# Issue order at the start of a fused RWKV-7 and gated-cosine kernel: loads, first chunks and one chunk's segments

## The chip, the core and the metric

The kernel runs on one core of one Trainium2 chip. Its metric is the device time of one execution, in microseconds (us). A core has TensorE for matrix products and transposes (PE in the profile, PEld for its weight loads), VectorE (DVE), ScalarE (ACT), GpSimd (POOL) and SyncE (SP, which here only issues DMA transfers). Each engine works through its own instruction list in program order, and engines wait for each other by semaphores.

## What is computed

A linear-attention recurrence over 768 tokens, and behind it a feed-forward layer with the activation h cos(h):

```python
batch, n_heads, seq, head_dim = (4, 8, 768, 40)
for t in range(S):
    y[:, :, t] = einsum('bhd,bhde->bhe', rt, state)
    Sa = einsum('bhde,bhe->bhd', state, at)
    state_decay = state * wt[:, :, None, :] - einsum('bhd,bhe->bhde', Sa, bt)
    state = state_decay + einsum('bhd,bhe->bhde', vt, kt)
# y, as 3072 tokens of 320 numbers, is x
h = x @ w_in            # 320 x 2048
g = h * cos(h)
out = g @ w_out         # 2048 x 320
```

All inputs r, k, v, w, a, b are float32; the two weight matrices arrive as 64-bit numbers.

## The kernel before

The sequence is cut into 24 chunks of 32 tokens; a chunk of all four batches fills 128 partitions. Inside a chunk the recurrence is solved in closed form, from chunk to chunk a state `qz` is carried.

For a chunk c there are these pieces of work, each a function whose instructions are spread over the engines:

- `p1_w`, `p1_a`, `p1_b`, `p1_n` take chunks two at a time. They transpose w, a and b on TensorE (tiles wT, aps, bT), take running products of w (for the first four chunks by a scan on VectorE, later from a scan over four chunks, `ws_scan`, that goes through DRAM as `wd`), divide b by w (`over_w`: a reciprocal on VectorE, a product into `bn` on GpSimd) and form the products of a and b (nps, evacuated to `nt`).
- Every four chunks a triangular inverse is taken from `nt` on VectorE in many short steps (tiles `inv`, `inv_tmp`, `u`). `inv` is first filled on GpSimd with zeros and a diagonal of -1. For chunks 0 to 7 it is inverted as two diagonal blocks, and `pair_first`, `pair_second` add the off-diagonal block with TensorE (tile below).
- `p2_in` and `p2_kn` copy v, r and k of a chunk into padded tiles on GpSimd (vp, rp, kn, vvm); `p2_v`, `p2_k`, `p2_g` transpose them on TensorE (vT, kT) and form the gram products (gram).
- `ch_t`, `ch_q`, `ch_x`, `ch_s`, `ch_z` (t, q, x, s, z below) carry the state through the chunk: transposes of it (sT), products (qps, x0ps, sps, dps) and in z its update and the output yt. `tokens` stores yt to DRAM (xd) and fetches it back transposed (xT) for the feed-forward layer.
- The feed-forward layer runs over pairs of chunks and quarters of the 2048 columns: `first_a`, `first_b` (tile ph), then the cosine (turns, gT), and `second` (tile po). These pieces are put between the others wherever a segment list has M.

The weights are first turned from 64-bit to 32-bit numbers in 20 blocks of 128 x 512 (`rounded`): a fetch of 512 KB (words), `taken` (L243, L244 on VectorE, L247, L249 on ScalarE), `mantissa` (L253 on VectorE, L256 on ScalarE) and `product` (L259 on VectorE, a sign product L262 on GpSimd). These are queued as `w_steps`, four for each block.

The order of everything is written out by hand. `step(work, of_inv, of_w)` runs a segment, then what `later(n, ...)` had set to follow n steps on (mostly loads), then so many inverse steps and weight steps. `busy(n)` and `kept_busy(n)` issue products of zeros on TensorE that nobody reads. The last part of the kernel is one loop over chunks with a list `segs` for each; before it stands the start, chunks 0 to 3, as straight code.

All loads in question go out on SyncE's queue. A load of one input of one chunk is four DMAs of 40 KB in rows of 160 bytes. k, v and r have one tile each, so the loads of chunk c + 1 wait for the copies of chunk c on GpSimd (`landed`); w, a and b alternate between two tiles from chunk 4 on. A DMA on this queue also waits for the one that used the same of eight semaphores before it.

The lines that matter for the change and the prediction, in the start:

Of the kernel before, what the change touches and what calls it, by code (L numbers as in the profile page):

```python
# [9 lines left out]
F32 = mybir.dt.float32  # L10
# [10 lines left out]
def kernel(  # L21
# [43 lines left out]
    nc = tc.nc  # L65
# [269 lines left out]
    G = {"rest": []}  # L335
# [98 lines left out]
    def p1_n(c):  # L434
        ps = at("nps")
        for i in range(2):
            for j in range(4):
                for bb in range(B):
                    for e in range(2):
                        mm(  # L440
                            ps[blk[bb ^ e], e, (4 * i + j) * C : (4 * i + j + 1) * C],
                            G["bT", c + i][half[e], j, blk[bb]], G["aT", c + i][half[e], j, blk[bb]],
                            i == 0 and j == 0,
                        )

        if c % 4 == 0:
            G["nt"] = sb1.tile([P, C, 4, 2, HH], F32, tag="nt", name="nt")
            if c < 8:
                G["noff"] = sb2.tile([P, 4, 2, HH, C], F32, tag="rt", name="noff")
        for e in range(2):  # L450
            nc.scalar.copy(
                G["nt"][:, :, c % 4 : c % 4 + 2, e, :].rearrange("p t c j -> p c j t"),
                ps[:, e, : 2 * HH * C].rearrange("p (c j t) -> p c j t", c=2, j=HH),
            )
        if c < 8:
            for e in range(2):
                nc.scalar.copy(
                    G["noff"][:, c % 4 : c % 4 + 2, e, :, :].rearrange("p c j t -> p c (j t)"),
                    ps[:, e, : 2 * HH * C].rearrange("p (c n) -> p c n", c=2),
                )  # L460
        if c % 4 == 2:
            G["inv"] = sb1.tile([P, C * C], F32, tag="inv", name="inv")
            nc.gpsimd.memset(G["inv"], 0.0)
            nc.gpsimd.memset(G["inv"][:, :: C + 1], -1.0)


    def inv_start():

# [397 lines left out]
    def p1(c):  # L866


        def first_w():
            p1_w(c)  # L870
            if c == 4:
                later(1, lambda: load(6, "w"))

        def both_a():
            p1_a(c)
            if c == 4:
                later(1, lambda: load(7, "w"))
                for i in range(2):
                    later(1, lambda i=i: load(6 + i, "ab"))
            elif c > 4 and c + 3 < NCH:  # L880
                for m in range(6):
                    later((9 if c == 6 else 2) + m, lambda m=m: load(c + 2 + m % 2, "wab"[m // 2]))

        return [first_w, both_a, lambda: p1_b(c), lambda: p1_n(c)]
# [8 lines left out]
    def p2(c):  # L893
        def last():
            p2_g(c)
            if c + 1 < NCH:
                later(1, lambda: p2_in(c + 1))

        return [lambda: p2_v(c), lambda: p2_k(c), last]

# [8 lines left out]
    with tc.manual_schedule():  # L909
# [56 lines left out]
        first, other = p1(0), p1(2)  # L966
        for seg in first[:2]:
            step(seg)
        load(4, "ab")
        load(5, "a")  # L970
        for seg in (*other[:2], *first[2:], *other[2:]):
            step(seg)
        for m in range(2):
            w_work[m][0]()
        scanned(1)
        p2_in(0)
        p2_kn(0)
        inv_steps.extend(by_blocks(0))
        v, k, g = p2(0)
        v1, k1, g1 = p2(1)  # L980
        x0, s0, z0 = main(0)[2:]
        for n, seg, idle_n in ((6, v, 0), (0, k, 0), (0, g, 4), (4, x0, 6), (2, v1, 5)):
            for _ in range(n):
                inv_steps.pop(0)()
            step(seg)
            if seg is x0:
                w_work[2][0]()
                p2_kn(1)
            busy(idle_n)
# [5 lines left out]
        step(g1)  # L995
        busy(3)
        N_PAD = {0: 0, 19: 75}
        step(lambda: pair_first(0, 0, False))
        for m in range(3, 5):
            w_work[m][0]()  # L1000
        step(lambda: pair_second(0, 0, False), 0, 1)
        step(s0, 0, 3)
        busy(6)
        step(z0, 0, 4)
        busy(4)
        for n, c, name in ((3, 4, "w"), (5, 5, "w"), (7, 5, "b")):
            later(n, lambda c=c, name=name: load(c, name))
# [19 lines left out]
        for c in range(NCH):  # L1027
            t, q, x, s, z = main(c)
            v, k, g = p2(c + 1) if c + 1 < NCH else [lambda: None] * 3
            q0 = c - c % 4 + 4  # L1030
            fill, pn, pn4 = (1, 4), None, None
            if c == 0:
                segs = []
            elif c == 1:
                segs, fill = [t, F1, v, q, k, S1, x, g, s, z], (1, 4)
            elif c == 2:
                segs, fill = [t, F2, v, q, S2, k, M, x, M, F3, g, M, s, S3, M, z, M, M], (0, 2)
            elif c == 3:
                pw4, pa4, pb4, pn4 = p1(4)
                pw, pa, pb, pn = p1(6)  # L1040
                segs = [
                    t, pw4, M, q, pa4, M, x, lambda: scanned(2), M, s, pw, M, pb4, pa, M, pn4, M, z, M,
                    pb, v, pn, k, M, g,
                ]
                fill = (2, 3)
            elif c == 4:
                pw, pa, *p8 = p1(8)
                firsts = [lambda n=n: pair_first(4, n) for n in range(4)]
                seconds = [lambda n=n: pair_second(4, n) for n in range(4)]
                F4, F5, F6, F7 = firsts  # L1050
                S4, S5, S6, S7 = seconds
                segs = [
                    t, v, M, q, M, k, x, M, F4, M, S4, F5, M, s, F6, M, pw, F7, M, z, M, g, M, pa, S5, lambda: scanned(3),
                ]
                fill = (2, 0)
            elif c == 5:
                pw, pa = p1(10)[:2]
                pb, pn = p8
                segs = [t, M, pb, q, M, pn, k, M, x, M, s, S6, M, pw, v, M, z, S7, M, g, M, pa, M]
            elif c % 4 == 0 and q0 < NCH:  # L1060
                pb, pn = p1(q0)[2:]
                segs = [t, v, M, q, M, k, x, M, g, M, s, pb, M, z, M, pn, M, M]
                if q0 + 4 < NCH:
                    segs.insert(-1, lambda: scanned(c // 4 + 2))
            elif c % 4 == 1 and q0 < NCH:
                pw, pa = p1(q0 + 2)[:2]
                segs = [t, M, pw, q, M, x, k, M, s, v, M, z, M, pa, M, g, M, M]
            elif c % 4 == 2 and q0 < NCH:
                pb, pn = p1(q0 + 2)[2:]
                segs = [t, M, pb, q, M, pn, v, M, x, M, s, k, M, g, M, z, M, M]  # L1070
            elif c % 4 == 3 and q0 + 4 < NCH:
                pw, pa = p1(q0 + 4)[:2]
                segs = [t, M, pw, q, M, x, k, M, s, v, M, z, M, pa, M, g, M, M]
            else:
                segs = [t, v, M, q, M, x, k, M, g, M, s, M, M, z, M, M]
            n = len(segs)

            goal = 8 * (c + 1) - (18 if c < 19 else 20)
            empty, places = 0, segs.count(M)
            if c > 3:  # L1080
                empty = max(0, min(places - (goal - done), 2 if c < 8 else places))
                goal = max(goal, done + places - empty)
            place = 0
            if c == 19:
                shifted(N_PAD[c])
            for i, seg in enumerate(segs):
                kept_busy(FILL.get((c, i), 0))
                while seg is s and ("rt", c) not in G:
                    if allowed(c):
                        piece(4, 0)  # L1090
                    else:
                        inv_steps.pop(0)()
                while seg is pn4 and w_steps:
                    w_steps.pop(0)()
                if seg is not M:
                    step(seg, *((0, 0) if c < 3 and seg in (*firsts, *seconds) else fill), small=seg in (q, x, g, s, z, pn, pn4, *firsts, *seconds))
                    if seg not in (*firsts, *seconds) and (c < 2 or c == 2 and not done):
                        busy({s: 6, q: 5, v: 4, k: 4, z: 4}.get(seg, 3))
                else:
                    place += 1  # L1100
                    if place * empty // places > (place - 1) * empty // places:
                        continue
                    if allowed(c) and (c != 4 or done < 23):
                        piece(*fill)
                while i == n - 1 and c > 3 and done < goal and c != 4 and allowed(c):
                    piece(*fill)
                if seg is pn and (c == 3 or c > 4 and c % 4 == 2):
                    inv_steps.extend(by_blocks(q0) if c == 3 else inverse(q0))
# [36 lines left out]
```

## Time and profile before

| | us |
|---|---|
| median of three runs | 814.49 |
| lowest and highest | 811.71, 815.9 |
| the profiled execution | 814.53 |
| its span in the trace | 812.8 |
| TensorE busy in the span | 758.7 (93%) |
| VectorE, ScalarE, GpSimd busy | 485.8, 387.1, 199.4 |
| granted TensorE clock, mean | 0.975 |

The span is what the trace covers; the execution is 1.7 us longer. Times in the profile are from the span's start. The page's row of DMA queues:

```profile
q1 hardware_dynamic: 180560, 51.95, 29.5%
q8 instruction: 140, 2.29, 1.2%
```

Columns: packets, megabytes, share of the time of 16 DMA engines. A row of a timeline gives start, length, engine, line, operation, tile written and tiles read, shape and count; in brackets stands how long the engine had been idle before, and who released it. A row of a table of stretches gives the stretch, its length, busy time and number of instructions of each engine, then the granted TensorE clock, the DMA share and GB/s.

### The profile page before, as it was taken

Reading aid. Unit: us, or ns where it says so; the run is one execution under the profiler, and the core shown is the slowest. Engines: PE = TensorE matmul, PEld = TensorE weight load, DVE = VectorE, ACT = ScalarE, POOL = GpSimd, SP = SyncE. Lnnn points to the kernel's source line nnn. Section 1 sums busy time; section 2 is a strip of 40 time slices with the busy share of each in tenths; the row PEclk is TensorE's granted clock in tenths of the full one; section 3 lists DMA queues with packets and bytes.
Section 4 is the critical chain, followed back from the end, with each engine's and each line's share of the span. In section 5 each row is a group of like instructions: output and inputs, shape, how many; then the busy total and the mean of one; then the engine's idle time right before and its main releaser. Section 6 shows DMA issues by size and latency. Waiting matters only on the chain.

```text
span 812.8 us, 39682 instructions
## 1 busy us (share of the span) xinstructions
PE 758.7 (93%) x17859; PEld 582.0 (72%) x17859; DVE 485.8 (60%) x1025; ACT 387.1 (48%) x723; POOL 199.4 (25%) x354
## 2 busy tenths in 40 slices
PE   3678799799999999999999999999999999999997
PEld 2545477677777777777777777777777777777775
DVE  6948858855743797553895554994346873332231
ACT  1326577454454346446436535534635445363352
POOL 5215634330404230230330330331130222201000
PEclk9878699999999999999999999999999999999999
DMA  8656553344244324324214314223220212101000
GB/s 123 120 142 170 158 141 99 54 114 67 51 94 92 67 42 72 69 89 70 59 36 74 78 47 71 55 45 68 45 45 21 45 37 57 23 14 36 19 17 16
DMA packets 183304, 55.79 MB, mean 69 GB/s; under 512 B 157152, under 2 KB 178656, under 8 KB 183136
## 3 DMA queue, kind: packets, MB, share of 16 engines
q1 hardware_dynamic: 180560, 51.95, 29.5%
q8 instruction: 140, 2.29, 1.2%
q10 hardware_dynamic: 2320, 0.98, 0.6%
q0 software_dynamic: 256, 0.33, 0.2%
q14 instruction: 28, 0.23, 0.1%
HBM read 42.07 MB, written 11.14 MB: 65 GB/s over the span
## 4 chain that ended last, share of the span: by engine, by line
PE 68%; DVE 15%; DMA 4%; issue 4%; ACT 4%; SPq 3%; POOL 1%; DVEq 0%; ACTq 0%; POOLq 0%
PE ph L101 23%; PE po L101 19%; PE x0ps L101 4%; PE dps L101 3%; DVE inv_tmp L478 3%; SPq L152 3%; PE gram L101 3%; DVE inv L482 3%; PE vT L328 2%; DVE rw L393 2%; PE sps L101 2%; PE busy L101 2%; PE nps L101 2%; PE qps L101 2%; PE sT L638 1%
## 5 line engine op out<-in xcount | busy, mean ns | idle before, releaser
L101 PE MATMUL po<-w_out_sb,gT 128*128 128x320 f32 x768 | 223.3, 439 | 0.0
L101 PE MATMUL ph<-xT,w_in_sb 128*128 128x256 f32 x768 | 186.7, 388 | 1.5 <-DMA xT<-xd 1.5
L101 PEld LDWEIGHTS po<-w_out_sb,gT 128*128 128x128 f32 x768 | 140.2, 190 | 54.2 <-issue 1.7
L101 PEld LDWEIGHTS ph<-xT,w_in_sb 128*128 128x128 f32 x768 | 140.5, 191 | 30.0 <-issue 10.6
L810 ACT ACTIVATE turns<-ph,rnd 128x512 f32<-128x512 f32 x96 | 64.1, 686 | 151.7 <-PE ph L101 151.3
L812 DVE SCALAR_TENSOR_TENSOR turns<-turns,ph 128x512 f32<-128x512 f32 x96 | 64.0, 684 | 116.0 <-ACT turns L810 115.8
L820 DVE TENSOR_TENSOR gT<-ph,turns 128x512 f32<-128x512 f32 x96 | 65.8, 686 | 37.8 <-ACT turns L817 37.8
L737 POOL TENSOR_TENSOR qz<-qz,wc 128x160 f32<-128x160 f32 x92 | 42.0, 475 | 158.5 <-DVE qz L736 157.9
L817 ACT ACTIVATE turns<-turns,half_pi 128x512 f32<-128x512 f32 x96 | 69.3, 722 | 3.1
L816 ACT ACTIVATE turns<-turns 128x512 f32<-128x512 f32 x96 | 60.1, 627 | 19.1 <-DVE turns L812 19.1
L101 PE MATMUL ph<-xT,w_in_tail 64*128 64x256 f32 x384 | 54.7, 402 | 0.0
L482 DVE TENSOR_TENSOR inv<-inv,inv_tmp 128x31 f32<-128x31 f32 (+15 forms) x124 | 51.2, 413 | 4.3
L570 POOL COPY vp<-nat_v 128x320 f32<-128x320 f32 x24 | 11.7, 489 | 164.4 <-DMA nat_v<-in_v_dram 121.1
L478 DVE TENSOR_TENSOR inv_tmp<-u,inv 128x31 f32<-128x31 f32 (+15 forms) x124 | 48.5, 391 | 2.3
L736 DVE TENSOR_TENSOR qz<-dps,qz 128x160 f32<-128x160 f32 x92 | 29.1, 316 | 33.3 <-PE dps L101 33.2
L393 DVE RECIPROCAL rw<-nat_w 128x320 f32<-128x320 f32 x20 | 42.8, 2142 | 0.0
L642 ACT COPY s<-sT 128x512 f32<-128x512 f32 x46 | 24.5, 585 | 37.8 <-PE sT L638 37.8
L101 PEld LDWEIGHTS ph<-xT,w_in_tail 64*128 64x128 f32 x384 | 33.3, 186 | 9.3 <-issue 5.6
L101 PEld LDWEIGHTS <-idle 32*64 32x64 bf16 (+2 forms) x443 | 21.5, 101 | 24.3 <-issue 19.7
L748 POOL TENSOR_TENSOR yt<-yt,wb 128x512 f32<-128x512 f32 x24 | 31.6, 1316 | 22.4 <-DVE yt L743 22.4
L702 DVE TENSOR_TENSOR sm<-sps,su 128x128 f32<-128x128 f32 x48 | 11.7, 285 | 34.1 <-ACT sm L697 31.3
L394 POOL TENSOR_TENSOR bn<-nat_b,rw 128x320 f32<-128x320 f32 x22 | 19.8, 900 | 48.5 <-DVE rw L393 38.5
(136 smaller groups left out, 1126.7 us busy)
## 6 DMA issues: line engine op xcount, KB each, us to landing
words<-in_moe_w_in_dram SPq DMA_DIRECT2D x8, 512.0 KB
nat_k<-in_k_dram SPq DMA_DIRECT2D x96, 40.0 KB
nat_v<-in_v_dram SPq DMA_DIRECT2D x96, 40.0 KB
nat_r<-in_r_dram SPq DMA_DIRECT2D x96, 40.0 KB
xd<-yt SPq DMA_DIRECT2D x48, 80.0 KB
out_dram<-ot SPq DMA_DIRECT2D x24, 160.0 KB
nat_b<-in_b_dram SPq DMA_DIRECT2D x88, 40.0 KB
nat_a<-in_a_dram SPq DMA_DIRECT2D x80, 40.0 KB
```

The source lines that it names most:

```text
L101: nc.tensor.matmul(o, lhsT=lhsT, rhs=rhs, start=start, stop=stop, skip_group_check=True)
L393: nc.vector.reciprocal(rw, wn)
L478: nc.vector.tensor_tensor(tmp, u[:, j : j + 1, :j].to_broadcast([P, C - j, j]), x[:, j:, j : j + 1].to_broadcast([P, C - j, j]), ALU.mult,)
L482: nc.vector.tensor_tensor(x[:, j:, :j], x[:, j:, :j], tmp, ALU.subtract)
L736: nc.vector.tensor_tensor(z, pick(dp, 0, (2 * N72 + C, 2), (N72, 2), (1, D)), z, ALU.add)
L737: nc.gpsimd.tensor_tensor(z, z, wc.rearrange("p (f m b) -> p f m b", f=2, m=2)[:, :, :, bb] .unsqueeze(3).to_broadcast([P, 2, 2, D]), ALU. ...
L748: nc.gpsimd.tensor_tensor(yt.rearrange("p j b t -> p (j b) t"), yt.rearrange("p j b t -> p (j b) t"), wx, ALU.mult)
L810: nc.scalar.activation(n, u, ACTF.Identity, bias=rnd, scale=1.0)
L812: nc.vector.scalar_tensor_tensor(n, n, -ROUND, u, ALU.add, ALU.subtract)
L816: nc.scalar.activation(n, n, ACTF.Abs)
L817: nc.scalar.activation(n, n, ACTF.Sin, bias=half_pi, scale=-2.0 * math.pi)
L820: nc.vector.tensor_tensor(gT[:, 2 * e : 2 * e + 2].rearrange("p f t -> p (f t)"), us[e], ns[e], ALU.mult)
```

## The change

It moves instructions and removes no computation. In the start:

- `load(4, "b")` and the fetches of the first two weight blocks are issued after the segment v of chunk 0, that is behind k, v and r of chunk 1 in SyncE's queue, instead of before.
- The filling of `inv` for chunks 0 to 3 becomes a function of its own and is called after `p2_in(0)` and `p2_kn(0)`, so GpSimd copies v, r, k of chunk 0 first.
- Six instead of four inverse steps stand before x of chunk 0 on VectorE.
- The first four steps after it take 2, 2, 4, 2 weight steps instead of 0, 1, 3, 4.
- `p2_in(2)` follows four steps after the gram of chunk 1 instead of one.

Further on, the loads of a for chunks 6 and 7 both go ahead of those of b, and in the list of chunk 5 the state update z stands before wT (pw) and vT (v), while pa follows g without a feed-forward piece between them. The number of pieces in the list is unchanged.

```diff
-        if c % 4 == 2:
-            G["inv"] = sb1.tile([P, C * C], F32, tag="inv", name="inv")
-            nc.gpsimd.memset(G["inv"], 0.0)
-            nc.gpsimd.memset(G["inv"][:, :: C + 1], -1.0)
+        if c % 4 == 2 and c > 2:
+            inv_space()
+
+    def inv_space():
+        G["inv"] = sb1.tile([P, C * C], F32, tag="inv", name="inv")
+        nc.gpsimd.memset(G["inv"], 0.0)
+        nc.gpsimd.memset(G["inv"][:, :: C + 1], -1.0)
...
-                for i in range(2):
-                    later(1, lambda i=i: load(6 + i, "ab"))
+                for n in "ab":
+                    for i in range(2):
+                        later(1, lambda n=n, i=i: load(6 + i, n))
...
-                later(1, lambda: p2_in(c + 1))
+                later(4 if c == 1 else 1, lambda: p2_in(c + 1))
...
-        load(4, "ab")
+        load(4, "a")
         load(5, "a")
         for seg in (*other[:2], *first[2:], *other[2:]):
             step(seg)
-        for m in range(2):
-            w_work[m][0]()
         scanned(1)
         p2_in(0)
         p2_kn(0)
+        inv_space()
...
-        for n, seg, idle_n in ((6, v, 0), (0, k, 0), (0, g, 4), (4, x0, 6), (2, v1, 5)):
+        for n, seg, idle_n in ((6, v, 0), (0, k, 0), (0, g, 4), (6, x0, 6), (2, v1, 5)):
             for _ in range(n):
                 inv_steps.pop(0)()
             step(seg)
+            if seg is v:
+                for m in range(2):
+                    w_work[m][0]()
+                load(4, "b")
...
-        step(lambda: pair_first(0, 0, False))
+        step(lambda: pair_first(0, 0, False), 0, 2)
         for m in range(3, 5):
             w_work[m][0]()
-        step(lambda: pair_second(0, 0, False), 0, 1)
-        step(s0, 0, 3)
+        step(lambda: pair_second(0, 0, False), 0, 2)
+        step(s0, 0, 4)
         busy(6)
-        step(z0, 0, 4)
+        step(z0, 0, 2)
...
-                segs = [t, M, pb, q, M, pn, k, M, x, M, s, S6, M, pw, v, M, z, S7, M, g, M, pa, M]
+                segs = [t, M, pb, q, M, pn, k, M, x, M, s, S6, M, z, M, S7, M, pw, v, M, g, pa, M]
```

## The prediction

> **What bounds the kernel now.** I read the page first (TensorE busy 93% of the span), then the stretches, to see where the other 7% sits:
>
> ```profile
> 36.00:66.00 30.00, 20.91 (x583) 11.64 (x570) 14.96 (x42) 6.71 (x14) 4.19 (x7) 0.75 0.62 162
> 66.00:110.00 44.00, 36.33 (x969) 23.71 (x968) 38.48 (x70) 30.31 (x54) 26.72 (x27) 0.82 0.59 157
> 150.00:165.00 15.00, 11.56 (x226) 8.54 (x226) 11.76 (x20) 5.53 (x11) 4.05 (x9) 0.89 0.46 75
> 235.00:254.00 19.00, 16.08 (x400) 12.97 (x399) 9.72 (x19) 7.36 (x13) 6.51 (x15) 1.00 0.41 94
> 254.00:812.00 558.00, 549.62 (x12307) 425.43 (x12305) 311.75 (x686) 265.86 (x494) 109.45 (x195) 1.00 0.24 49
> ```
>
> Columns: stretch, length, busy TensorE, weight load, VectorE, ScalarE, GpSimd, clock, DMA. From 254 us on TensorE rests 8.4 us in 558: nothing there for this change. It rests 9.1 us in 36 to 66, 7.7 in 66 to 110, 3.4 in 150 to 165, 2.9 in 235 to 254: 23 us at most, plus what a clock below 1.00 costs. Next the chain of waits in the start, and SyncE's queue beside it:
>
> ```profile
> 34.51 7.22 DMA words<-in_moe_w_in_dram
> ...
> 42.12 1.33 SPq L152
> ...
> 44.48 1.99 DMA nat_r<-in_r_dram
> ...
> 46.62 0.46 POOL rp L570
> ...
> 47.13 0.66 PE vT L328 x4
> ```
>
> ```profile
> 33.95 0.92 SPq L235 DMA_DIRECT2D words<-in_moe_w_in_dram  x2
> 34.98 2.33 SPq L152 DMA_DIRECT2D nat_k<-in_k_dram  x4
> 37.41 4.66 SPq L152 DMA_DIRECT2D nat_v<-in_v_dram  x4
> 42.12 2.81 SPq L152 DMA_DIRECT2D nat_r<-in_r_dram  x4
> ```
>
> The program gives SyncE's DMAs eight semaphores in turn, so one waits for the DMA eight places ahead: v of chunk 1 stands behind the two 512 KB word blocks until they land, and TensorE waits for v and r. Then TensorE's timeline at the three other places:
>
> ```profile
> 40.62 1.10 PE L101 MATMUL x0ps<-vvm,ag 32*32 32x72 f32 x62 [2.43 <-issue]
> 76.24 0.63 PE L328 MATMUL kT<-ident,kn 128*128 128x128 f32 x4 [1.69 <-POOL w_in_tail L262]
> 160.02 0.72 PE L328 MATMUL aps<-ident,nat_a 128*128 128x128 f32 x4 [1.57 <-DMA nat_a<-in_a_dram]
> 160.53 3.53 PE L101 MATMUL ph<-xT,w_in_sb 128*128 128x256 f32 x8
> 242.87 0.72 PE L101 MATMUL below<-rt,half 32*32 32x16 f32 x64 [1.44 <-DVE yt L743]
> 252.73 1.99 PE L101 MATMUL ph<-xT,w_in_sb 128*128 128x256 f32 x8 [1.48 <-DMA xT<-xd]
> ```
>
> The bracket is the idle time just before. Each is a wait that this change touches; the eight ph matmuls at 160.53 take 3.53 us against 1.99 elsewhere.
>
> **What the Trainium skill says.** "Runtime: NRT & Kernel Launch", Instruction fetch mechanics: an engine's instructions come by DMA in blocks of 16 KiB (256 instructions), mostly hidden. The page's q8 row agrees in size (140 packets, 2.29 MB: 16 KB each); hidden it is not here: the 2.43 us of "issue" before x0ps fall where the word blocks move (DMA 315 GB/s in 36 to 38). That a fetch was late there is my reading, not shown. "TensorE: Matmul & The Clock Gate", What's actually happening: an idle window of about 3.4 us halves the clock; here it is 0.50 from 161 to 163, after TensorE was busy 1.9 of the 4 us before 160. "SBUF — State Buffer", SBUF: two separate sides: VectorE with two SBUF inputs and GpSimd lock each other out for an instruction; here `mant` L243 takes 0.42 us alone and 1.38 beside GpSimd's sign product.
>
> **The change part by part.**
>
> 1. *Start, SyncE.* b of chunk 4 and the two word blocks go behind k, v, r of chunk 1. a of chunk 5 is issued at 29.37 (where b was) to 31.96, k to 34.4, v to 36.8 (k's pace of 2.43, as nothing large is ahead), r to 39.2 with v's 2.43 or r's 2.81. r landed 1.5 us after its last issue before (46.47 against 44.93), so it lands near 41, and GpSimd's copy (0.45) is over by 41.5. TensorE comes to vT at 44.39 in any case; the rp half starts one half (0.66) later at 45.05 in place of 47.13: 2.08 us. k, v, r's own wait is for GpSimd's chunk 0 copies: the two inv memsets (0.96 + 0.15) go behind these, so they end near 30.3, before k at 31.96. The memsets then end by 31.5, VectorE first needs inv at 34.35: free, uncovered it is 1.1 us. Words land near 46.5, VectorE first reads them at 52 or later: free. b of chunk 4 is needed at 142: free. Behind the words in the queue: the store of the scan, word tails, k, v, r of chunk 2; all in the same places, about 1 us earlier.
>    The fetch stall of 2.43 now lies before the word blocks. Bounds: none of it to all of it goes; I take 0.9. Part: 3.0 (1.5 to 4.5).
> 2. *VectorE.* Two more inverse steps (four operations at some 0.31 pitch, 1.25 us) before the copy of x0 fill its 1.50 idle there. The inverse ends at 47.8, not 49.1; TensorE reaches `below` near 50.4, so it isn't late next. Nothing gained, nothing lost; the copy ends within 0.3 us of before.
> 3. *Weight steps.* Two, two, four, two with the first four steps of chunk 0 where there were none, one, three, four: ten against eight. A block of words has four steps (product, fetch, mantissa, taken), so all later steps keep their number, but their phase moves by half a block. Behind sps, a busy of 2.7 us hides the extra work. In chunk 1 ScalarE's copies of s, vT and q then stand behind a mantissa (L256, 0.72, after VectorE's L253, 0.68 to 0.97) rather than behind expo and sign (L247 and L249, 1.37, after L243 and L244, 1.8 when slowed). VectorE has, up to the copy of x0, one L253, L243, L244 and L259 fewer (0.97 + 1.49 + 0.41 + 0.68 = 3.55). vp and rp of chunk 2 (0.9) move behind qz and yt on GpSimd; before they waited for DMA at 55 and 58, ahead of a sign product. vT comes at 70.06, GpSimd would be ready near 70.4 less the shift: 0 to 0.4 lost, under the wait for s. What TensorE can win to x0ps is its idle there, 0.54 + 1.69 + 0.24 = 2.47. Bounds: 2.5 won, 3 lost (a mantissa waits for a slowed VectorE in two steps). I take 1.5.
> 4. *Chunks 6 and 7.* The queue loses four DMAs of b ahead of a of chunk 7: 153.46 to 155.44, 1.98 us. It lands at 157.95 rather than 159.93. The first half of aps is bound by VectorE (157.79) and ends at 158.45: the 1.57 is gone whole, and bT's copies, next, are done. With TensorE idle 1.57 less, the eight ph matmuls may keep the full clock: 0 to 1.54; I take 0.8. b of chunk 6 lands 2 us later, near 160; its bT is at 172.74: covered by 12 us. Part: 2.4 (1.5 to 3.2).
> 5. *Chunk 5.* The state update z (with the piece between) goes ahead of wT, vT. dps comes at 235.1 in place of 239.75, VectorE's qz, yt follow at once, not behind L812 (1.2): the 1.44 before `below` goes. GpSimd's yt ends near 241 instead of 247.7, no longer behind b of chunk 10 (landed 243.98). The store of yt then stands behind SyncE's b and ws (to 244.12), so xT comes at 244.1 + 4.96 (252.73 less 247.77) = 249.1. TensorE gets there near 250: the 1.48 goes too. But next is bn of chunk 11: aT 1.2, reciprocal 2.14, bn 0.86 after aps. VectorE frees at 249.2 (gram's masks), so bn ends near 253.4 and the second half of bT starts there, against 255.0. Part: 1.6 (0.3 to 2.9).
>
> Sum: 3.0 + 1.5 + 2.4 + 1.6 = 8.5. The profiled execution took 814.53 (span 812.8 and 1.7 around it); 806.0. The median of the runs shown, 814.49, is the same to 0.04, so no correction. A run-to-run spread of 4 us in these three runs is as large as two of the parts.
>
> **Rivals.**
>
> A. All four parts hold: 806.0, as worked out. For it: each wait has its named releaser, and each releaser's own cause is moved. Chance 0.58.
>
> B. What the start wins is taken back by VectorE's conversion of words, which is busy 38.5 of 44 us in 66 to 110 and 100% in 130 to 140; only parts 4 and 5 remain: 814.5 - 4.0 = 810.5. Against it: the phase leaves VectorE less to do before x0, and 110 to 128 has TensorE without gaps but VectorE with many. Chance 0.22, half on each side of the bound.
>
> C. The change doesn't do what it says: the fetch stall moves to `below` or gram with the word blocks and takes the 2.1, and a of chunk 7 is late from VectorE's reciprocal (149.55) ahead of w of chunk 7. Only part 5: 813. Chance 0.05.
>
> D. Slower: on ScalarE each of chunk 1's eight filled steps has its state copy behind a mantissa that waits for VectorE: 0.72 + 0.68 + 0.05 = 1.45 a step, 11.6 in all, against 7.0 won elsewhere: 819. It decides from 7.0 / 8 = 0.9 a step. For it: kT's 1.69 is such a wait (vT's copies ran at 75.04 to 76.10). Against it: expo and sign stood there before at a higher price. Chance 0.15.
>
> **How the numbers follow.** The likeliest is A: 806.0, its own range 800 to 810. The range 800 to 813 takes in B and C; outside lie D and a full win of all bounds. A measurement of this kernel can tell about 0.5% (4.1 us) from no change, so faster means below 810.4: 0.58 + 0.12 = 0.70; within: 0.10 + 0.05 = 0.15; slower 0.15.
>
> **What would show it.** Part 1: no wait for vp or rp before vT of chunk 1, gram of chunk 1 near 49 instead of 51.4. Part 3: kT's wait short, x0ps of chunk 1 near 75 instead of 79.24. Part 4: no DMA wait before aps of chunk 7, and the ph after it at 1.99. Part 5: no wait before `below` and ph, but one before the second half of bT. Wrong it is if "issue" before TensorE grows by more than 3 us in 36 to 110, or the shift of the start isn't seen at the first po (130.19).

## The result, and the profile after

The changed kernel takes 811.33 us in the median of 20 runs, the kernel before 813.9 in runs taken between them: a ratio of 0.9969, 95% interval 0.9951 to 0.9987. That is 2.5 us won (1.1 to 4.0), where 8.5 were forecast. A second set of runs of the same kernel gave 0.9976 (0.9957 to 0.9994). The profiled execution after took 810.8 us, span 809.1.

The table of stretches, from the trace after (columns as before):

```profile
36.00:66.00 30.00, 23.61 (x762) 14.31 (x742) 22.00 (x56) 10.12 (x20) 8.54 (x13) 0.77 0.75 204
66.00:110.00 44.00, 36.25 (x1013) 22.99 (x1017) 34.35 (x58) 29.04 (x52) 24.82 (x24) 0.84 0.57 143
150.00:165.00 15.00, 14.64 (x327) 11.49 (x326) 12.66 (x27) 7.66 (x16) 4.19 (x10) 1.00 0.53 103
235.00:254.00 19.00, 17.23 (x338) 13.56 (x338) 8.87 (x11) 8.40 (x16) 6.86 (x14) 1.00 0.39 86
```

TensorE's rest has shrunk from 9.1 to 6.4 in the first stretch and from 3.4 to 0.4 in the third, but in 66 to 110 it is as before (7.7). The start did what was meant. SyncE's queue and TensorE's timeline after:

```profile
31.43 3.07 SPq L152 DMA_DIRECT2D nat_k<-in_k_dram  x4
34.59 1.87 SPq L152 DMA_DIRECT2D nat_v<-in_v_dram  x4
36.51 2.79 SPq L152 DMA_DIRECT2D nat_r<-in_r_dram  x4
39.35 0.92 SPq L235 DMA_DIRECT2D words<-in_moe_w_in_dram  x2
```

```profile
39.03 1.10 PE L101 MATMUL x0ps<-vvm,ag 32*32 32x72 f32 x64
...
41.36 0.60 PE L328 MATMUL vT<-ident,vp 128*128 128x128 f32 x4
41.80 0.65 PE L328 MATMUL vT<-ident,rp 128*128 128x128 f32 x4
```

r of chunk 1 is issued by 39.3, not 44.9, nothing stands in brackets before x0ps and vT, and s of chunk 0 starts 4.6 earlier than before. Then the waits that took the place of the old ones, all in TensorE's timeline after:

```profile
89.62 0.32 PE L101 MATMUL dps<-idle 32*64 32x288 bf16 x4 [3.30 <-DVE sm L704]
...
154.30 1.09 PE L328 MATMUL aps<-ident,nat_a 128*128 128x128 f32 x8 [0.36 <-DVE sm L704]
...
173.25 0.49 PE L101 MATMUL gram<-aT,kT 40*32 40x32 f32 x36 [1.40 <-issue]
...
231.45 0.77 PE L101 MATMUL dps<-vvm,kn 32*40 32x72 f32 x53 [1.78 <-issue]
...
235.46 0.48 PE L101 MATMUL ph<-xT,w_in_tail 64*128 64x256 f32 x1 [1.45 <-issue]
```

The DMA wait before aps of chunk 7 is gone (154.30 is all eight transposes in one row). A 3.30 wait for the mask of s stands in chunk 1, and stalls marked "issue" (an idle time for which the profile names no other engine and no transfer) stand inside gram of chunk 4, dps and ph of chunk 5, none of which had one in the kernel before. The lead on the trace of before is 4.6 (s of chunk 0), 5.8 (x0 of chunk 1), 2.4 (first po, 127.77 against 130.19), 6.9 (dps of chunk 3), 6.0 (s of chunk 5), 3.4 (aps of chunks 10 and 11): the gains appear where they were forecast, and each is partly lost soon after.

### The profile page after: what moved, and what is told of

Its sections match the earlier page's. It is cut to its first block, busy times and chain, and to the rows that moved or that the text cites. A ratio compares the mean times of both kernels' runs of the same rounds, so it can differ in the third digit from the quotient of the medians.

```text
span 809.1 us, 39677 instructions
## 1 busy us (share of the span) xinstructions
PE 757.2 (94%) x17859; PEld 579.9 (72%) x17859; DVE 486.5 (60%) x1025; ACT 387.5 (48%) x723; POOL 200.9 (25%) x354
## 4 chain that ended last, share of the span: by engine, by line
PE 68%; DVE 17%; ACT 5%; issue 4%; DMA 3%; POOL 2%; SPq 1%; DVEq 0%; POOLq 0%; ACTq 0%
PE ph L101 24%; PE po L101 19%; PE dps L101 4%; PE x0ps L101 4%; DVE rw L393 3%; PE gram L101 3%; DVE inv_tmp L480 3%; PE vT L328 2%; DVE inv L484 2%; PE sps L101 2%; PE nps L101 2%; PE qps L101 2%; PE kT L328 1%; PE sT L640 1%; PE bT L328 1%
## 5 line engine op out<-in xcount | busy, mean ns | idle before, releaser
L628 ACT COPY vvm<-gram 128x256 f32<-128x256 f32 x24 | 8.8, 369 | 45.6 <-DVE ag L623 45.2
```

## The experiments

Every kernel was timed beside the kernel before, and profiled once. A difference of two medians is good to some 2 us at best, so I also compare stretches between landmarks in the profiles. In the texts below, gram of chunk 4, dps of chunk 5 and so on are the places in TensorE's timeline, and a lead is how much earlier than in the first trace of before TensorE gets there.

### Take parts away from the change

Two edits against the changed kernel set chunk 5's list and the weight steps back to those of the kernel before; the runs below use one, the other or both:

```diff
-  segs = [t, M, pb, q, M, pn, k, M, x, M, s, S6, M, z, M, S7, M, pw, v, M, g, pa, M]
+  segs = [t, M, pb, q, M, pn, k, M, x, M, s, S6, M, pw, v, M, z, S7, M, g, M, pa, M]
```

```diff
-        step(lambda: pair_first(0, 0, False), 0, 2)
+        step(lambda: pair_first(0, 0, False))
...
-        step(lambda: pair_second(0, 0, False), 0, 2)
-        step(s0, 0, 4)
+        step(lambda: pair_second(0, 0, False), 0, 1)
+        step(s0, 0, 3)
...
-        step(z0, 0, 2)
+        step(z0, 0, 4)
```

The change again, unaltered:

> The changed kernel once more, on the chip of the next three. In its first trace TensorE is 7.2 us ahead of the kernel before at dps of chunk 1, 1.6 at aps of chunk 4, 6.0 at sps of chunk 5, 3.4 from chunk 6 to the end, and loses 1.78 and 1.45 us to late instructions in chunk 5's state update. If these are properties of the program, they return within 1 us each and the time is 811 (808.5 to 813). If they are chance of one execution, the stalls in chunk 5 are elsewhere or gone and the shifts differ by more than 2 us.

Measured: 811.83, ratio 0.9976. The start and the wait of 3.3 for the mask of s came back (3.29). The stalls came back in part: 0.79 in gram of chunk 4 for 1.40, 1.18 in the tail of ph for 1.45, and none in dps of chunk 5, where the first profile had 1.78. A wait of 0.69 for DMA stood before the second half of aps of chunk 7. So the size of a stall is a draw, and one profile of a kernel does not show that a stall has gone.

Old chunk 5 list alone:

> The changed kernel with the segment list of chunk 5 as before. Theory F (the state update's 128 small products now follow sps and below closely, TensorE uses up 256 instructions faster than they arrive, and the two stalls of 1.78 and 1.45 cost more than the removed waits): the lead of 6.0 us before chunk 5 stays to the end, the time is 2.6 us below the changed kernel, about 808.7. Rival, the prediction's part 5 (the reorder wins 1.6 and something else in chunk 5 lost it): the lead falls to under 3 us in chunk 5 here too and the time is 1.6 us above the changed kernel, about 813.

Measured: 809.93, ratio 0.9948 (0.9928 to 0.9968); no stall in dps of chunk 5, and the 1.44 before `below` is back. In its profile, 3.4 above its median, the lead was 3.3 at s of chunk 5 and 1.6 at aps of chunks 10 and 11, so the 6.0 of the theory did not last, and the time lies nearer to the theory than to the rival.

Only the start (loads, inv, inverse steps; all else as before):

> Only the start's moves: k, v, r ahead of b and words, inv filled later, two more inverse steps ahead of x; weight steps, p2_in of chunk 2, chunks 5 to 7 as before. Theory W (the half block by which the weight steps moved is what gave back 5.6 us between dps of chunk 1 and aps of chunk 4): TensorE is 4 to 5 us ahead at s of chunk 0 and still 4 or more ahead at aps of chunk 4; the time is 810. Rival Q (VectorE's weight blocks and the words' DMAs set the pace of chunks 1 to 3 whatever the phase): 4 to 5 ahead at s of chunk 0, 2 or less at aps of chunk 4, time 812 to 813.

Measured: 811.08, ratio 0.9960 (0.9942 to 0.9978), that is 3.3 won (1.8 to 4.7). Its aps of chunk 7 waits 1.24 for DMA. The lead was 5.0 at s of chunk 0 and 3.2 at aps of chunk 4, between the two expectations.

Old weight steps alone:

> The changed kernel with 0, 1, 3, 4 weight steps in the start as before. Theory W: the wait of 3.3 us before dps of chunk 1 for the masked sps goes, TensorE is 5 us or more ahead of the kernel before at aps of chunk 4 (1.6 in the changed kernel), and the time is 2 to 3 us below the changed kernel, about 808.5. Rival Q: the lead at aps of chunk 4 is again 1 to 2.5 and the time that of the changed kernel within 1 us.

Measured: 810.36, ratio 0.9970 (0.9950 to 0.9990): no longer than the changed kernel, and without its 3.30 wait in chunk 1. The lead at aps of chunk 4 was 3.6, again between the two expectations.

Both old (the start, the later copies of chunk 2 and a ahead of b remain):

> The changed kernel with the weight steps 0, 1, 3, 4 and chunk 5's list of the kernel before; the load order of the start, the later copies of v and r of chunk 2 and the order of a and b remain. Theory (each part counts for itself; the start wins about 2.7, a ahead of b 2.4, the weight steps cost 1.2 to 1.5 and chunk 5's new list 1.7): 808.7 against 813.8 of before, ratio 0.994, under the changed kernel by 2.5 to 3; no wait of 3.3 for the mask of s before dps of chunk 1, no wait of VectorE for words of more than 0.5 before 110, no instruction stall in dps of chunk 5. Rival (the medians' differences overlap, what one part wins another takes): 810.5 to 811.5, no better than either of the two undone alone.

Measured: 811.14, ratio 0.9980 (0.9962 to 0.9998). The sum of the parts' medians fell: this kernel is no better than those two. The wait for the mask of s is 1.61.

### Add one part to the kernel before

A second profile of the kernel before, to see what of its waits comes back:

> The kernel before once more, for a second profile of it. Theory (what differs between the variants' profiles is mostly the code): the stretches between landmarks repeat those of the first profile within 0.5: s of chunk 0 near 57, 22 from there to x0 of chunk 1, 62.8 to aps of chunks 4 and 5, 15.8 to aps of 6 and 7, 10.4 to dps of chunk 3, 21.4 from x0 to aps in chunk 5; ratio 1.000. Rival (much of what the prediction counted as costs of before was one draw): s of chunk 0 at 55 to 56, aps to dps near 8.4, since the half clock at 161 doesn't come back.

Measured: 812.58, ratio 1.0007 (0.9987 to 1.0028). From s of chunk 0 on, four of the first five stretches came back within 0.5: 21.9, 62.3, 15.8, 10.5, the fifth (58.8) within 1.0; the DMA wait before aps (1.81) and the low clock there too. So these waits belong to the code. The start was later by 1.4, and x0 to aps in chunk 5 took 23.1, not 21.4: such sizes are a draw.

Only a ahead of b:

> The kernel before with a of chunks 6 and 7 ahead of b and nothing else. Prediction's part 4: 2.4 won, 811.4 against 813.8, ratio 0.997; aps of chunk 7 without its 1.57 of DMA wait, the ph after it at 1.99 rather than 3.53. Rival: only the DMA wait goes, the clock stays low: 1.0 won, 812.8; or nothing of it lasts: 813.8.

Measured: 811.39, ratio 1.0005 (0.9984 to 1.0026). The wait is gone and aps to dps takes 7.0, not 10.4; but the time doesn't show it (the rival's "nothing of it lasts").

Only the weight steps:

> The kernel before with the weight steps 2, 2, 4, 2 and nothing else. Theory from the traces so far (what the steps win up to x0 of chunk 1 is given back while VectorE's mask of s and the words are late, and part of it comes back before aps of chunks 6 and 7): 2 less than before from s of chunk 0 to x0 of chunk 1 (20 to 21 rather than 22 to 23), 3 to 5 more from there to aps of chunks 4 and 5 (66 to 67 rather than 62.8), 1.9 less from there to aps of 6 and 7 (13.9); no change in sum, 812 to 814, with a wait of 2.5 to 3.3 for the mask of s before dps of chunk 1. Prediction's part 3: 1.5 faster. Rival D of the prediction: 2 or more slower.

Measured: 811.58, ratio 1.0003 (0.9978 to 1.0028). The stretches are 20.0, 64.6 and 13.8: less, more, less, as expected. Their sum is 98.4, against 98.6 to 100.8 in the four profiles with the old loads and the old steps, and the time shows nothing of it. The wait for the mask of s is only 0.71 here, not 2.5 to 3.3. With early loads and new steps together it is 2.5 to 3.3 in six profiles of eight, and 1.0 and 0.7 in the other two; with the old steps it is 0 to 1.8 in eight profiles.

The stretches of all 17 profiles, sorted by what they contain (mean in us, range, number of profiles):

| stretch (start to start) | without the part | with it |
|---|---|---|
| span's start to s of chunk 0: load order | 56.7 (55.5 to 58.4, 5) | 52.6 (50.9 to 54.7, 12) |
| to x0 of chunk 1: weight steps, new loads only | 23.6 (22.8 to 24.3, 4) | 21.1 (20.3 to 21.8, 8) |
| to aps of 4, 5: weight steps, new loads only | 63.0 (61.2 to 64.5, 4) | 66.6 (64.8 to 70.3, 8) |
| to aps of 6, 7: weight steps | 15.3 (14.0 to 15.8, 8) | 13.7 (13.0 to 13.9, 9) |
| to dps of chunk 3: a ahead of b | 9.4 (8.1 to 10.5, 4) | 7.3 (7.0 to 8.0, 13) |
| to x0 of chunk 5: a ahead of b | 59.4 (58.8 to 59.8, 4) | 60.6 (59.0 to 62.1, 8) |
| x0 to aps in chunk 5: its new list | 22.2 (21.4 to 23.1, 11) | 23.4 (21.8 to 24.2, 4) |

Left out in the last two rows are the runs below that move a transfer or the instruction blocks there. The ranges of the last two rows overlap. Row 2 with the old loads is 21.6 (4 profiles, old weight steps): of the 4.1 that the loads win, 2 are gone by x0 of chunk 1.

### Why the lead in chunk 1 doesn't last

ScalarE and VectorE in the changed kernel, around the mask of s:

```profile
87.94 0.64 ACT L249 ACTIVATE sign<-words 128x512 bf16<-128x512 int32 x1
88.48 0.47 ACT L699 COPY sm<-sps 128x160 f32<-128x160 f32 x2
...
88.98 0.49 DVE L704 TENSOR_TENSOR sm<-sps,su 128x128 f32<-128x128 f32 x2 [0.89 <-ACT sm L699]
```

and with the old weight steps:

```profile
88.20 0.72 ACT L256 ACTIVATE mant<-mant,by_out 128x512 f32<-128x512 f32 x1
88.83 0.47 ACT L699 COPY sm<-sps 128x160 f32<-128x160 f32 x2
...
89.33 0.49 DVE L704 TENSOR_TENSOR sm<-sps,su 128x128 f32<-128x128 f32 x2 [1.22 <-ACT sm L699]
```

TensorE starts sps at 81.66 in the first and at 85.61 in the second, yet sm comes at 88.98 and 89.33. ScalarE has from 82.3 on a chain of mantissa, exponent and sign of the word blocks, each behind a step of VectorE (its brackets name mant and expo), and the copy of s stands behind it. A lead of 4 us is swallowed. Over the profiles, sm starts at 88.6 in the mean with the early loads and old weight steps (four) and at 89.2 with the new ones (eight): what the steps win before x0 never gets past sm.

A second candidate was the queue of the words: in the changed kernel VectorE waits 1.86 for them near 92. The load of b of chunk 5, just ahead of six fetches, set ten steps later:

```diff
-        for n, c, name in ((3, 4, "w"), (5, 5, "w"), (7, 5, "b")):
+        for n, c, name in ((3, 4, "w"), (5, 5, "w"), (17, 5, "b")):
```

> The changed kernel with the load of b of chunk 5 set to follow ten steps later. Theory (SyncE's queue makes the words late: six word fetches stand behind v, r of chunk 2 and b of chunk 5, and b takes 1.94 of it): VectorE's wait for words near 92, 1.9 in the changed kernel and 3.4 in its second run, falls to 0 to 1.5; the time is 0 to 1 better than the changed kernel, 810.5 to 811.5. Rival (words wait for the blocks' own buffers, so that the queue doesn't matter): the wait stays at 1.9 to 3.4 and the word fetches are issued at the same time.

Measured: 809.35, ratio 0.9978 (0.9954 to 1.0002). The wait for words is gone (it is 0.40 to 3.44 in the six profiles with the same start and b in its old place), and the six fetches go out at 86.35 instead of 88.03, so the queue was its cause; the time is that of the changed kernel within the error, and the wait for sm stays at 2.48. With the old list of chunk 5 too:

> The changed kernel with chunk 5's list of the kernel before and with the load of b of chunk 5 ten steps later. Theory (both were better than the changed kernel alone, by 1.9 and about 1): ratio 0.992 to 0.995, 808 to 809.5 where before has 813; no wait for words in 66 to 150, no stall in dps of chunk 5. Rival (these differences are draws): 0.996 to 0.998.

Measured: 809.06, ratio 0.9956 (0.9939 to 0.9972), between the two expectations; against the theory, VectorE now waits 2.54 for words near 118 instead. This edit is worth nothing that can be told.

### What the "issue" stalls are

Chunk 5's stalls are 3.2 us in the first profile of the changed kernel and 1.2 in the second. The block of 256 TensorE instructions (128 products and their weight loads) was moved by half a block in chunk 5 only, with 64 tiny products ahead of chunks 5 and 6:

```diff
+            if c in (5, 6):
+                for _ in range(64):
+                    mm(G["po", 0][:1, DM : DM + 1], idle[:, :1], idle[:, :1], False)
```

> The changed kernel with 64 products of one row and one column (into a column of po that nobody reads) put ahead of chunk 5, and 64 ahead of chunk 6, so that in chunk 5 alone every block of 256 TensorE instructions begins half a block earlier in the program. Theory (the two stalls in chunk 5 are a block of instructions that comes late): the stalls leave the 8th product of vvm and kn and the 8th product of w_in_tail; the blocks now begin inside below and near the 8th product of sm and bn in dps, so the stall, if any, is there, 0.5 to 2 us in all rather than 3.2. The extra products cost some 0.7 us each, so the time is 811 to 812. Rival (the stalls belong to what dps reads or writes, and the profile only names them issue): they stay at the same products with 3.2 us, the time is 1.5 longer, 813.

Measured: 809.59, ratio 0.9961 (0.9942 to 0.9980). TensorE's timeline with the blocks moved:

```profile
228.79 0.53 PE L101 MATMUL below<-rt,half 32*32 32x16 f32 x41 [1.10 <-issue]
229.25 1.99 PE L101 MATMUL ph<-xT,w_in_sb 128*128 128x256 f32 x8
...
231.32 0.82 PE L101 MATMUL dps<-vvm,kn 32*40 32x72 f32 x60
...
233.10 1.14 PE L101 MATMUL ph<-xT,w_in_tail 64*128 64x256 f32 x8
```

The stalls have left dps and ph; one of 1.10 stands 64 products earlier, with 41 of the 64 products of `below` still to go. That is the place of the block's edge, not of any tile. The time is lower than both expectations had it.

The traces show the late blocks directly too, as they hold each packet of q8, the queue for instructions. All are of 16,384 bytes. There are 140 in every other profile, which at 256 instructions each is 35,840, where TensorE ran 17,859 products and as many weight loads (35,718 in all); and there are 141 in this one:

```profile
q8 instruction: 141, 2.31, 1.1%
```

The 128 products added, with their weight loads, are 256 instructions: one block. In the changed kernel two packets end at 229.92 and 233.95, and TensorE goes on behind the two stalls at 231.45 and 235.46; with the blocks moved, one ends at 227.43 and TensorE goes on at 228.79. Over all 17 profiles TensorE has 169 waits of 0.4 us or more named "issue". In 162 of them it goes on 1.1 to 1.6 us after a packet of q8 has ended; of its other waits of that length from 30 to 240 us, 25 in 195 do. (The seven exceptions stand before kT of chunk 0.) So these stalls are blocks of instructions that come late. The 2.43 before x0ps, which the prediction read so without showing it, is one: its packet ends at 39.10, and TensorE goes on at 40.62.

What makes a block late is told by moving transfers. In chunk 5, the store of a scan of w:

```diff
-        later(2, lambda: ws_store(q))
+        later(9 if q == 3 else 2, lambda: ws_store(q))
...
-            later(12, lambda: ws_fetch(q + 1))
+            later(14 if q == 2 else 12, lambda: ws_fetch(q + 1))
```

(the second edit is for chunk 4, below)

> The changed kernel with the same load of w behind xT, and with the store of the next scan (0.66 MB) set to follow 9 steps later rather than 2, behind the eight loads of b of chunks 10 and 11; chunk 5's new list stays. Theory (the store that moves 227 GB/s in 226 to 230 delays the block of instructions in dps of chunk 5): the stall after the seventh product of vvm and kn, 1.78, 1.18, 0.99 and 0.41 so far, is under 0.3, and that in the tail of ph (1.45) stays or grows, since the store now stands beside it; none in gram near 173. Time 809 to 811. Rival (a block takes 4 to 5 whatever moves beside it): both stalls stay.

Measured: 808.09, ratio 0.9960 (0.9933 to 0.9987), not to be told from the changed kernel. The stretch 226 to 230 in the changed kernel (first fence), and the same with the store moved, then dps and ph in its timeline:

```profile
226.00:230.00 4.00, 3.67 (x152) 2.98 (x151) 0.68 (x3) 0.49 (x2) 0.00 (x0) 1.00 0.81 227
```

```profile
226.00:230.00 4.00, 3.95 (x190) 3.27 (x184) 0.68 (x3) 0.49 (x2) 0.00 (x0) 1.00 0.38 63
```

```profile
228.94 1.11 PE L101 MATMUL dps<-vvm,kn 32*40 32x72 f32 x60
...
233.01 0.48 PE L101 MATMUL ph<-xT,w_in_tail 64*128 64x256 f32 x1 [1.18 <-issue]
```

With 63 instead of 227 GB/s beside it there is no stall in dps; the one in the tail of ph, beside eight loads of b, stays. That alone proves little, since the second profile of the changed kernel, where the store is not moved, has none in dps either:

```profile
226.00:230.00 4.00, 4.00 (x140) 3.16 (x139) 0.68 (x3) 0.49 (x2) 0.00 (x0) 1.00 0.68 200
```

```profile
227.45 0.40 SPq L180 DMA_DIRECT2D wd<-ws  x1
...
230.65 0.98 PE L101 MATMUL dps<-vvm,kn 32*40 32x72 f32 x60
```

The packets tell the two apart. Counting 128 products back from the edge in dps gives the time at which TensorE enters the block before. From there to the start of the next packet it is 2.8 us in the first profile (the store went out 0.5 before the entry) and 1.0 with the store moved, but also 1.0 in the second profile, where the store went out only at the entry. The four profiles with the new list and the store in its place have stalls of 1.78, 0.99, 0.41 and none. So the block is late where the store is well ahead of it, and whether it is ahead changes from run to run. x0 to aps takes 23.6 to 24.2 in the three with a stall in dps and 21.8 without; with the store moved it takes 22.0. The block in front of the tail of ph, in the run with the store moved, lasts TensorE some 2.6 us, counted in the same way, and TensorE goes on with the next one 3.7 after its entry, with loads of 40 KB beside it: there TensorE's pace is part of the cause.

Now chunk 4, where a ahead of b loses what it won: the load for the next scan of w put behind the fetch of xT (the second edit above), on the kernel with a ahead of b alone:

> The kernel before with a of chunks 6 and 7 ahead of b (as in the run of that alone), and with the load for the next scan of w set to follow 14 steps later rather than 12, which puts it behind the fetch of xT in SyncE's queue. Theory (that load of 0.66 MB delays a block of TensorE's instructions in gram of chunk 4): the stall of 1.56 in gram near 173 goes, to under 0.4; DMA in the 4 us before it falls from 185 to under 100 GB/s; 1 to 2 better than a ahead of b alone. Rival (TensorE takes the block's predecessor too fast in any case, whatever the DMA does): the stall stays at 1 to 1.7.

Measured: 811.21, ratio 0.9987 (0.9961 to 1.0013); the 1 to 2 us can't be told from nothing. First a ahead of b alone, a row of its table and one of its timeline; then the same with the load moved:

```profile
168.00:172.00 4.00, 3.65 (x115) 2.60 (x104) 2.02 (x5) 2.30 (x6) 1.40 (x4) 1.00 0.55 185
```

```profile
173.21 0.49 PE L101 MATMUL gram<-aT,kT 40*32 40x32 f32 x36 [1.56 <-issue]
```

```profile
168.00:172.00 4.00, 4.00 (x169) 3.05 (x156) 1.92 (x5) 2.40 (x6) 1.50 (x4) 1.00 0.22 61
```

```profile
171.41 0.72 PE L101 MATMUL gram<-aT,kT 40*32 40x32 f32 x62
```

Gram starts at the same time in both (171.32 and 171.41), and the stall is gone with the transfer. The other profiles bear this out. Of the nine with a ahead of b and the load in its old place, six have this stall (0.79 to 1.75) and three don't; none of the four with the load moved has it. From TensorE's entry into the block before to the start of the packet it is 2.3 to 3.4 us in the six, and 0.8 to 1.4 in the other seven. dps of chunk 3 to x0 of chunk 5 takes 60.5 to 62.1 in the six, 59.0 in two of the three (the third has the extra products ahead of chunk 5), and 59.1 to 60.3 with the load moved. So the transfer makes this stall, in most runs and not in all. In the kernel before, gram starts at 178.90; the load is issued at 169.56 there and has passed by then (61 GB/s in 176 to 180). Moving it in the changed kernel with the old list of chunk 5, and then with the old weight steps as well:

> The changed kernel with chunk 5's list of the kernel before and with the load for the next scan of w behind the fetch of xT (14 steps rather than 12, for that scan alone). Theory (a ahead of b is worth its 2 only where gram of chunk 4 isn't then kept waiting for instructions): dps of chunk 3 to x0 of chunk 5 takes 59 to 59.5 rather than 60 to 62, no stall in gram near 173 over 0.4; 1 to 2 better than the changed kernel with the old list, 807 to 809 where before has 812.6 to 813.8, ratio 0.992 to 0.995. Rival (a stall taken away here comes back at a later block of instructions, or the time is set elsewhere): 0.995 to 0.997.

Measured: 808.05, ratio 0.9943 (0.9918 to 0.9968); dps of chunk 3 to x0 of chunk 5 takes 59.3. The time does not differ from that of the same kernel without the moved load (0.9948).

> As the first of these three, with the weight steps 0, 1, 3, 4 of the kernel before. Theory (the new weight steps are worth nothing either way): within 0.2% of the first, 807 to 809.5. Rival (they cost 1.2 to 1.5, as the medians of the first call had it): 1.2 to 1.5 better than the first.

Measured: 807.80, ratio 0.9933 (0.9914 to 0.9952): 5.4 won. Its interval lies below that of the same kernel without the moved load (0.9962 to 0.9998), but the 3.8 us between the two are more than the 1.69 of the stall there, and the like step on the new weight steps shows no difference that can be told (0.9943 against 0.9948): what the moved load is worth stays open. dps of chunk 3 to x0 of chunk 5 took 60.3 here, as a stall of 1.25 stood at a later block (in `below`, near 190), which is the rival of the run before. This kernel beats the kernel before, and the changed kernel's interval overlaps only at its edge. The weight steps make no difference beyond the error, as expected.

## Why the forecast was too large

The sign and the range held; the likeliest case, A, did not. The sum failed because parts 3, 4 and 5 were each booked at the waits near the change and not followed far enough past them. Rival B's 810.5 comes near the 811.3, but by luck: B keeps parts 4 and 5 and gives up the start, while it is the start that lasts by itself (3.3). Point by point:

1. **Start, 3.0 (1.5 to 4.5).** Right: 3.3 alone, and 4.1 earlier at s of chunk 0. The order of SyncE's queue was the cause of the wait for v and r. The stall before x0ps went with it (1.6 to 3.5 in four of the five profiles with the old order, 0.5 in one of the twelve with the new); x0ps was over 1.6 earlier, so 0.9 for that was low.
2. **Inverse steps, nothing.** Nothing contradicts it; not tried alone.
3. **Weight steps, 1.5 won.** The step that failed is "what TensorE can win to x0ps is its idle there": it won that (2.4 in row 2), but the sum stopped at x0. Behind it the mask of s waits for ScalarE's and VectorE's conversion, and 3.6 are given back in row 3, 1.6 won in row 4. Alone: 0.2 lost, 1.8 won to 2.3 lost. This is the mechanism of rival B, the conversion that is busy in 66 to 110, with ScalarE in it besides VectorE; what was held against B, that the phase leaves VectorE less to do before x0, is true and doesn't help behind x0. Of D I found only this one place: the wait is 3.3, not 1.45 at each of eight steps.
4. **a ahead of b, 2.4.** The term "the 1.57 is gone whole" and the 0.8 of clock held locally (2.1 in row 5). What failed is "b lands later: covered by 12 us" as the only cost: gram of chunk 4 came 7.6 earlier, the 0.66 MB load of w (128 x 1280 words) only 3.3, so the two met in most runs, and 1.2 went back in row 6. Alone it was worth nothing: 1.3 won to 2.1 lost.
5. **Chunk 5, 1.6.** The term failed: nothing was won that can be told. The failed step is "next is bn of chunk 11" as the only thing that follows. The wait before `below` went, dps came at 229.2 rather than 235.1, and bn of chunk 11 was next with 0.87, as forecast. But z straight behind `below` and ph makes a run of small products that uses a block of instructions up in some 3.5 us (from the 24th product of sps, near 226.2, to 229.67), beside a transfer of 227 GB/s. Row 7 has 1.2 lost, not 1.6 won, and without a stall in dps the new list is at 21.8 and 22.0, within the old one's 21.4 to 23.1. The times alone don't settle it: with the new list 2.3 are lost in one pair (0.9976 against 0.9948) and 0.8 won in the pair with old weight steps (0.9970 against 0.9980).

Rows 1 to 7 for the whole change, with row 2 for both (21.6 to 21.1) and row 3 from the old kernel's 62.6: -4.1 - 0.5 + 4.0 - 1.6 - 2.1 + 1.2 + 1.2 = -1.9, beside -2.5 and -1.9 measured. The test named in the prediction, the shift at the first po, showed it: 2.4 there instead of 4.5 from parts 1 and 3. What stays open is the split of row 3 between late masks, late words and stalls of instructions: these come together, and only the words' wait was taken away by itself.

## What to carry to other kernels

Hold a stall named "issue" against the packets of the instruction queue, and count instructions to the edge of a block: in this kernel such a stall is a block that is late, and a large transfer that goes out just before TensorE enters the block ahead of it makes it so. Such stalls come and go from run to run, so take several profiles before calling one cured. A gain at one engine's wait lasts only to the next place where the chain passes through an engine with queued side work, so follow the sum past that copy before booking it. And each piece of work that comes earlier should be checked against the transfers that it now meets.

## What was unexpected in the hardware

The prediction cited the Trainium skill ("Runtime: NRT & Kernel Launch", Instruction fetch mechanics) for blocks of 256 instructions whose fetch is mostly hidden. The size agrees: each packet of q8 has 16,384 bytes, and 256 instructions more made one packet more. Hidden it is not for runs of 32-row products: each profile has five to eight such stalls of 0.7 to 3.8 us up to 131 us, at fixed places such as 27 products before the end of `below` or 26 before that of x0ps. Their sizes vary: the one in `below` of chunk 0 is 1.59 to 3.83 in eight profiles whose code is the same up to there. These eight reach s of chunk 0 at 50.9 to 54.7, in the main later where that stall is longer, so single profiles of like kernels differ by up to 4 us in the start, in part through these stalls.

The clock followed some of them. After the stalls of 1.56, 1.69 and 1.75 in gram of chunk 4 it fell, to 0.72, 0.73 and 0.59 in the lower of the stretches 172 to 176 and 176 to 180; after those of 0.79, 1.28 and 1.40, and in the eleven profiles without one, it was 1.00 in both. The kernel with a ahead of b alone, where the stall is 1.56:

```profile
172.00:176.00 4.00, 2.66 (x111) 2.25 (x111) 1.74 (x7) 0.72 (x2) 0.00 (x0) 0.85 0.20 53
176.00:180.00 4.00, 4.00 (x48) 3.43 (x50) 3.55 (x14) 1.80 (x4) 0.00 (x0) 0.72 0.41 68
```

The Trainium skill ("TensorE: Matmul & The Clock Gate", What's actually happening), which the prediction used, names an idle window of about 3.4 us for the half clock. Here TensorE was busy 2.66 of the 4 us from 172 to 176, so a shorter rest was enough; what else counts is not shown.

The prediction's line on VectorE with two SBUF inputs does not cover its example, as L243 reads only words. What the trace shows is that the L243 of 75.04, beside GpSimd's sign product (74.60 to 76.13), took 1.37 and ended 0.3 after it.
